# A prime-factor transform (3 by 256) in place of the half-length one, in an attention kernel that ends in a spectral convolution

## The chip, the cores and the metric

The kernel runs on one core of one Trainium2 chip. The metric is device microseconds for one execution; the time of a kernel is the median of its runs. The core has five engines that work side by side and wait for each other by semaphores: TensorE (PE; its weight loads are listed as PEld), VectorE (DVE), ScalarE (ACT), GpSimd (POOL) and SyncE (SP, which here only issues transfers). Matmul results land in an accumulator memory of eight banks of 512 fp32 columns (the tile `space` in the rows), from which VectorE and ScalarE copy them out.

## The reference

Attention with two kinds of heads, then a gated convolution over the sequence, done with Fourier transforms. Cut to what is computed:

```python
scores = q @ k.T / sqrt(64)                    # batch 4, 8 heads, 768 rows, 64 wide, fp32
mask = causal for some heads, else causal & (first 4 keys | last 64 keys)
x = softmax(where(mask, scores, -1e9)) @ v     # heads side by side: [4, 768, 512]
x1, x2, x3 = split(x @ w_proj, 3)              # each [4, 768, 512]
conv = irfft(rfft(x2, axis=1) * rfft(filter_fft, axis=0), n=768)
out = (x1 * conv * x3) @ w_out                 # [4, 768, 512]
```

## The kernel before

The function `patterned` names every small piece of work (an "op") and runs them in the order of a long text, `FAST`. A word of that text gives the op, the accumulator bank it starts in (`@0` to `@7`) and, where there is a choice, its engine (`/v` VectorE, `/s` ScalarE, `/p` GpSimd). Each engine executes its own ops strictly in that order; nothing is planned at run time. (`general`, a second program for other patterns of heads, is not taken.)

Heads are worked in sixteen pairs, n = 0 to 15, four to a batch b. For a pair: `lk`, `lq`, `lv` load (SP), `ck`, `cq`, `cv` cast to bf16, `T` and `E` transpose (for n below `TURNED` on TensorE and copied out by `E`, else by an SP transfer), `sc` makes scores in chunks, `ex` the exponential (ScalarE), `at` multiplies with the values, `rec` and `nm` normalise. The masks come in one of two ways: for n below `BIASED_FAST` an op `sb` adds a large negative number by a matmul of the identity with a table before `ex`; for the other pairs `mk` (and `mr`) multiply the exponentials by 0 or 1 on VectorE or GpSimd.

The forward transform is done before the projection, since both are linear. `fd` and `fe` fold the 768 rows to halves of 384 (difference and sum), `fA`, `fS`, `fb`, `fr` fold each half by three, and `W` multiplies with cosine and sine tables. `We` copies the result into `xh`, and `X` multiplies it with the middle third of `w_proj`: the spectrum of x2 in three tiles t of two times 512 columns. `Xe` copies it out, and `pa`, `pb`, `pc` multiply it by the filter's spectrum `HAB` into `P`; the third tile needs its halves of the partitions swapped, which `sw` does by two SP transfers. The filter's own spectrum comes from `fold`, `F` and the scaled copies `H`, with two SP transfers (`Hd`).

The inverse transform `c` has, for each of four blocks of 128 channels (cb), two sums of three products of 384 columns, one for even and one for odd frequencies. `ce` copies the first out, and two `cv` add and subtract to the two halves of the rows. `g` is x1 times x3, `y` the gate with conv, `o` the output product, `oe` its copy, `st` its store. `x1`, `x3` are the other two thirds of the projection, from the transposed attention output `xT` (`tn`, `te`: by TensorE for the pairs in `TURNED_BACK`, else by an SP transfer), and `xs` copies x1 out. `blank` ops are products of zeros that fill TensorE's time early on; there are thirteen of them (`BLANKS`), 29 products in the main text and the first five ahead of it.

Of the kernel before, what the change touches and what calls it, by code (L numbers as in the profile page):

```python
# [9 lines left out]
FP32 = mybir.dt.float32  # L10
# [103 lines left out]
SIXTHS = (0, 1, 2, 3, 4, 5, 6, 7, 8, 9, 10, 11, 12, 13, 14, 15)  # L114
# [7 lines left out]
lflag lk0 lq0 lk1 lq1 mblank want tcol fcol0 table sin0 fcol1 blank0@6 tfrac quarter mtab0 par turns other angle  # L122
ident mtab1 wrap size sin cos
# [3 lines left out]
ones1 ones2 mtab3 blank5@0 lq2 lk2 blank10@1 ck0/v skew0/s lv0 parb skew1/p G32/s T0.1@2 xp0 cq0/v lk3 blank6@3  # L127
mtab2 E0.1/v lv1 blank8@4 Gk1/s lv3 blank7@5 Gm00 btab G31/p blank1@6 ck1/v kz1 lq3 T0.0@7 lk4 alt blank3@0 Gm2
cq1/s G30/p Gh0 lq4 T1.1@1 Gm01 kz0 lv2 E0.0/s G00/v T1.0@3 G01/p Gm1 cq2/s lk6 E1.1/v sc0.1@4 sb0.1 lq6 ck2/p
sc0.3@6 ex0.1 Gh1 E1.0/v sc0.4@0 ones0 kx1/p sb0.4 lk5 sb0.3 T2.1@2 ex0.4 kz2 lk7 sc0.0@4 E2.1/v lq5 cv0/p sb0.0  # L130
Gt1@3 ex0.3 lq7 blank2@0 kx2/v Gt2@1 Gk0/p ex0.0 lv6 T2.0@2 ks1/p Ge2/v ck3/p sc0.2@6 Ge1/s E2.0/v sc1.2@4 sb1.2
lfilt sb0.2 T3.1@0 ex1.2 sc0.5@2 Gt0@1 ex0.2 cv1/v sc2.3@4 E3.1/v lv4 vx1/p sb0.5 ex0.5 sc1.0@6 lw2.1 Ge0/v
sb1.0 ks2/s vs1/v at0.0@2 lw2.0 ex1.0 at0.1 cq3/v lw0.1 T3.0@0 ex2.3 kx3/v sc1.1@6 rec0 lw1.1 sb1.1 nm0/v cv3/s
blank11@1 ex1.1 sc2.1@4 fe0/p sb2.1 tn0@1 cq4/v E3.0/s at1.0@2 lw0.0 blank9@6 ex2.1 ks3/v sc2.4@6 ck4/v at1.1
# [24 lines left out]
o0.1.1 o0.0.0 lk15 mk9.0/v ex10.0 sc9.2@2 o0.0.1 mk9.1/v T12 x11.2.0@4 ex9.2 mk10.0/v x11.2.1 fb7/v oe0.1/s
# [1682 lines left out]
```

## Time and profile before

| | |
|---|---|
| Runs | 195.18, 189.86, 193.86 us; median 193.86 |
| Profiled execution | 190.27 us, its span 188.4 us |
| Mean granted TensorE clock | 0.985 |
| Busy: TensorE, VectorE, ScalarE, GpSimd | 176.5, 161.2, 145.6, 69.0 us |
| Transfers | 34.01 MB, mean 180 GB/s |

Times in the rows are microseconds from the start of the span; a row of groups gives line, engine, operation, output<-inputs, shapes, count, then busy time, mean ns of one instruction, and the idle time of the engine just before them with what ended it. A matmul's mean duration is longer than its share of time, because the next one starts while it drains; the distance of starts tells the pace.

### The profile page before, as it was taken

The page shows a single profiled execution, that of the slowest core. Times are in us where ns is not written, and L with a number is a line of the kernel's source. Part 1 is how long each engine was busy: PE and PEld are TensorE (multiplying, and loading weights), DVE is VectorE, ACT ScalarE, POOL GpSimd, SP SyncE. Part 2 cuts the span into 40 slices and gives each one's busy share as a digit, 9 for nine tenths or more (in the row PEclk, how much of TensorE's full clock was granted, in tenths as well). Part 3 has the DMA queues.
Part 4 walks back from the last instruction along what each step waited for, and adds up shares of the span by engine and source line. Part 5 has one row for each costly group of instructions (what it writes and reads, how often), then busy time and mean ns, then how long its engine had stood idle before and what let it go on. Part 6 is the DMA issues. An engine that isn't in the chain of part 4 may idle for free.

```text
span 188.4 us, 4493 instructions
## 1 busy us (share of the span) xinstructions
PE 176.5 (94%) x1694; PEld 103.4 (55%) x1694; DVE 161.2 (86%) x329; ACT 145.6 (77%) x210; POOL 69.0 (37%) x103
## 2 busy tenths in 40 slices
PE   7879999989998999999999999999999999999970
PEld 2437664647745563575555656655657765555530
DVE  6887799789889999999989999999899996499810
ACT  5787899999999999988989999696977332426360
POOL 5874785554322224670250460700650630000000
PEclk9978999999999999999999999999999999999997
DMA  4999999999999999999999989982162002312074
GB/s 152 330 274 279 208 197 236 270 286 251 213 202 225 215 185 166 233 219 213 202 233 228 228 221 238 250 87 56 60 98 111 3 2 111 135 36 111 11 286 157
DMA packets 78955, 34.01 MB, mean 180 GB/s; under 512 B 68306, under 2 KB 75218, under 8 KB 78930
## 3 DMA queue, kind: packets, MB, share of 16 engines
q1 hardware_dynamic: 75986, 30.81, 73.9%
q0 software_dynamic: 2944, 2.88, 9.1%
q8 instruction: 14, 0.23, 0.5%
q14 instruction: 11, 0.09, 0.2%
HBM read 24.64 MB, written 6.29 MB: 164 GB/s over the span
## 4 chain that ended last, share of the span: by engine, by line
PE 66%; ACT 14%; DVE 6%; DMA 5%; issue 3%; POOL 2%; SPq 2%; DVEq 0%; ACTq 0%; POOLq 0%
PE space L1655 18%; PE space L1712 11%; PE space L1620 8%; PE space L1452 7%; PE space L1685 7%; PE space L1516 6%; ACT f_pT L1471 4%; DMA f_qkT<-f_qk_bf 3%; ACT f_HAB L1274 3%; DMA f_v_f<-in_v_dram 2%; PE space L1465 2%; ACT f_qk_bf L975 2%; SPq L1383 2%; PE space L1569 1%; PE space L1571 1%
## 5 line engine op out<-in xcount | busy, mean ns | idle before, releaser
L1471 ACT ACTIVATE f_pT<-space 128x1024 bf16<-128x1024 f32 (+3 forms) x68 | 58.8, 917 | 6.1 <-PE space L1465 1.9
L1655 PE MATMUL space<-f_xT,f_wproj 128*128 128x384 bf16 x256 | 47.9, 326 | 0.1
L1655 PEld LDWEIGHTS <-f_wproj 128*128 128x128 bf16 x256 | 24.0, 98 | 17.1 <-issue 1.0
L1712 PE MATMUL space<-f_wout,r_gy 128*128 128x512 bf16 x96 | 24.7, 379 | 0.0
L1452 PE MATMUL space<-f_qkT 64*128 64x128 bf16 (+3 forms) x248 | 22.6, 253 | 1.1 <-DVE f_attn L1533 0.5
L1620 PE MATMUL space<-f_wproj,f_xh 128*128 128x512 bf16 x96 | 22.7, 379 | 0.1
L1685 PE MATMUL space<-f_Gi,r_P 128*128 128x384 bf16 x96 | 19.0, 326 | 0.7 <-ACT f_evs L975 0.3
L978 DVE TENSOR_TENSOR f_pT<-f_pT,r_mtab 128x1024 bf16<-128x1024 bf16 (+3 forms) x33 | 18.5, 583 | 0.8 <-ACT f_pT L1471 0.6
L975 ACT COPY f_o<-space 128x1024 f32<-128x1024 f32 (+1 forms) x12 | 9.9, 836 | 11.3 <-PE space L1712 11.2
L1516 PEld LDWEIGHTS <-f_pT 128*128 128x128 bf16 x472 | 16.7, 97 | 3.6 <-issue 0.9
L1516 PE MATMUL space<-f_v_aug,f_pT 128*128 128x65 bf16 x392 | 17.9, 193 | 0.6 <-ACT f_X L975 0.5
L1452 PEld LDWEIGHTS <-f_qkT 64*128 64x128 bf16 x248 | 10.3, 94 | 13.1 <-issue 10.4
L978 POOL TENSOR_TENSOR f_uv<-f_fo 128x256 bf16<-128x256 bf16 x12 | 9.1, 766 | 21.1 <-DVE f_fo L978 15.8
L1696 DVE TENSOR_TENSOR f_conv<-f_evs,space 128x384 bf16<-128x384 f32 x32 | 16.1, 545 | 0.6 <-PE space L1685 0.3
L975 ACT CAST f_xh<-space 128x768 bf16<-128x768 f32 x14 | 11.2, 808 | 4.9 <-PE space L1573 4.6
L1620 PEld LDWEIGHTS <-f_xh 128*128 128x128 bf16 x96 | 9.0, 98 | 10.0 <-issue 0.4
L1712 PEld LDWEIGHTS <-r_gy 128*128 128x128 bf16 x96 | 9.0, 98 | 8.9 <-issue 0.4
L1533 DVE TENSOR_TENSOR f_attn<-space,f_rec 128x768 bf16<-128x768 f32 x14 | 13.4, 955 | 0.4
L1685 PEld LDWEIGHTS <-r_P 128*128 128x128 bf16 x96 | 8.8, 97 | 7.4 <-issue 1.1
L978 POOL TENSOR_TENSOR f_fo<-f_attn 128x384 bf16<-128x384 bf16 x11 | 10.4, 960 | 2.4 <-DVE f_attn L1533 1.9
L975 ACT CAST f_X<-space 128x1024 bf16<-128x1024 f32 x8 | 8.2, 1020 | 2.8 <-PE space L1620 2.7
L978 POOL TENSOR_TENSOR f_pT<-f_pT,r_mtab 128x512 bf16<-128x512 bf16 (+1 forms) x6 | 6.8, 1146 | 9.1 <-ACT f_pT L1471 9.1
(136 smaller groups left out, 345.7 us busy)
## 6 DMA issues: line engine op xcount, KB each, us to landing
f_v_f<-in_v_dram SPq DMA_DIRECT2D x32, 192.0 KB, 4.7
out_dram<-f_o SPq DMA_DIRECT2D x9, 512.0 KB, 3.1
r_qk_f<-in_k_dram SPq DMA_DIRECT2D x10, 192.0 KB, 4.4
r_qk_f<-in_q_dram SPq DMA_DIRECT2D x10, 192.0 KB, 5.0
r_qk_f<-in_k_dram SPq DMA_DIRECT2D x4, 384.0 KB, 11.3
r_qk_f<-in_q_dram SPq DMA_DIRECT2D x4, 384.0 KB, 6.1
f_qk_f<-in_q_dram SPq DMA_DIRECT2D x4, 384.0 KB, 5.8
f_qk_f<-in_k_dram SPq DMA_DIRECT2D x4, 384.0 KB, 6.6
```

Of the source, the lines that this page charges most:

```text
L975: nc.scalar.copy(out=out, in_=in_)
L978: (nc.gpsimd if now["engine"] == "p" else nc.vector).tensor_tensor(out, a, b, op)
L1274: nc.scalar.activation(out=out_(), in_=in_(), func=AF.Copy, scale=w / S)
L1452: nc.tensor.matmul(sc[:, bank, col:col + 128 * cnt], lhsT=keys, rhs=qkT(n)[rows, 0, 128 * i:128 * (i + cnt)], start=(col == 0 or not biase ...
L1471: nc.scalar.activation(out=pT(n)[:, c, :, 0:w], in_=held[f"sc.{n}.{c}"][:, :, 0:w], func=AF.Exp, scale=SCALE)
L1516: nc.tensor.matmul(att[:, hh, 65 * i:65 * i + 65], lhsT=pT(n)[:, c, bank, col:col + 128], rhs=values, start=(z == 0), stop=(z == len(here) ...
L1533: nc.vector.tensor_mul(attn(n).rearrange("p i hh d -> p hh i d"), rows[:, :, :, 0:64], held[f"rec.{n}"][:, :, :, None].to_broadcast([128, ...
L1620: nc.tensor.matmul(ps[:, u, :], lhsT=xh(b)[:, cc, chain, 128 * part:128 * part + 128], rhs=wproj()[:, cc, DM:2 * DM], start=(cc == 0), sto ...
L1655: nc.tensor.matmul(ps[:, s, 0:HS], lhsT=wproj()[:, cc, part * DM + cb * 128:part * DM + (cb + 1) * 128], rhs=xT(b)[:, cc, s * HS:s * HS + HS],
L1685: nc.tensor.matmul(ps[:, 0, 0:HS], lhsT=P(b)[:, t, u, ch], rhs=Gi()[:, tile_no], start=(m == 0), stop=(m == 2))
L1696: fn(conv[:, half * HS:half * HS + HS], held[f"evs.{b}.{cb}"], held[f"c_ps.{b}.{cb}.1"][:, 0, 0:HS])
L1712: nc.tensor.matmul(ps, lhsT=gy(b)[:, cb, i * 128:(i + 1) * 128], rhs=wout()[:, cb, :], start=(cb == 0), stop=(cb == NC - 1))
```

## The change

The two-halves structure of the inverse goes. The 768 rows are now seen as 3 by 256: row 3t + s belongs to class s, and the transform over 3 and the one over 256 are done one after the other. The pieces:

- `c` has three sums (one for each class) of two products of 256 columns, from six rows that new ops `q` recombine out of `P`: `qa`, `qs`, `qz`, `qb`, `qp`, `qm` (two inputs, 1024 elements), `qr`, `qh`, `qd` (scalings). `ce` and the sums `cv` go. For batches 0 to 2 (`DIRECT`) `y` reads the accumulator; for batch 3 one `cv` copies it to bf16 first, on ScalarE.
- Even and odd frequencies lie in separate halves of the partitions, so `sw` goes, and `xh` holds six groups of 128. The tables are made for this order of rows: `Gi` directly from cosines and sines instead of by transposes (`Gt`, `Ge`).
- The filter goes the way of the data: `fAF`, `fSF`, `fbF`, `frF`, products `K`, copies `Ke`, and transposes `F`; `HAB` is scaled out of these. `Hd` goes.
- x1 and x3 are read from the accumulator by class (a step of three), and outputs are stored to every third row.
- `BIASED_FAST` rises from 4 to 8: pairs 4 to 7 are masked by `sb` matmuls instead of `mk`. `TURNED_BACK` loses pair 14.
- `BLANKS` has nine entries: eight products of zeros fewer. A one-element GpSimd copy, `gate`, stands ahead of the filter's and weights' loads. The whole text `FAST` is in another order (not shown).

```diff
-TURNED_BACK = (0, 1, 2, 3, 4, 5, 6, 7, 14, 15)
+TURNED_BACK = (0, 1, 2, 3, 4, 5, 6, 7, 15)
-BIASED_FAST = 4
+BIASED_FAST = 8
-BLANKS = (5, 2, 2, 2, 2, 2, 2, 2, 2, 2, 2, 2, 2)
+BLANKS = (5, 2, 2, 2, 2, 2, 2, 2, 2)
+DIRECT = ((0, 0), (0, 1), (0, 2), (0, 3), (1, 0), (1, 1), (1, 2), (1, 3), (2, 0), (2, 1), (2, 2), (2, 3))
...
+    @op("gate")
+    def _():
+        nc.gpsimd.tensor_copy(out=buf("gate", [1, 1], FP32), in_=held["qk_f32.3"][0:1, 0, 0, 0, 0:1])
...
+    def spectrum(ps, u, uv, br, ch):
+        nc.tensor.matmul(ps[:, u, 0:256], lhsT=br[:, 1, u, ch], rhs=G()[:, 3 * u:3 * u + 2], start=True, stop=False)
+        nc.tensor.matmul(ps[:, u, 0:256], lhsT=uv[:, 2 * u, ch], rhs=Gk()[:, u], start=False, stop=True)
+        nc.tensor.matmul(ps[:, u, 256:384], lhsT=br[:, 0, u, ch], rhs=G()[:, 3 * u + 2], start=True, stop=True)
+
+    def sorted_(x, ps):
+        ev(x.rearrange("p g (u j) -> p u g j", u=2), ps[:, :, 0:HS].rearrange("p u (g j) -> p u g j", g=6))
...
+    sixths("F", fold, uvF, brF)
+    for cc in range(NC):
+        for u in range(2):
+            @op(f"K{cc}.{u}")
+            def _(cc=cc, u=u):
+                spectrum(banks(f"K_ps{cc}"), u, uvF(), brF(), slice(128 * cc, 128 * cc + 128))
...
+    for t in range(3):
+        @op(f"F{t}")
+        def _(t=t):
+            ps = banks(f"F_ps{t}", BF16, 1)
+            for c, g in enumerate(SPECTRUM[t]):
+                for cc in range(NC):
+                    nc.tensor.transpose(ps[:, 0, DM * c + 128 * cc:][:, 0:128], Hx()[:, cc, g], identity())
...
-        for half in range(2):
-            @op(f"sw{b}.{half}")
...
-                nc.sync.dma_start(out=Xw[to], in_=held[f"X.{b}.2"][at])
+        # qa: SD[0:2] = P1 + P2     qs: SD[2:4] = P1 - P2     qr: row 0 of SD = 2 * row 0 of four P rows
+        # qh: Y0 = P0 / 2           qz: Y0 += SD[0, 3]        qd: SD[1:3] *= sqrt(3)
+        # qb: P0 -= SD[0, 3]        qp: P[2:4] = P0 + SD[1:3] qm: P[4:6] = P0 - SD[1:3]
...
-                ev(buf(f"x1s.{b}.{cb}", [128, 2, HS], BF16, tag), held[f"x1_ps.{b}.{cb}"][:, :, 0:HS])
+                ev(buf(f"x1s.{b}.{cb}", [128, 3, 2, 128], BF16, tag), classes(held[f"x1_ps.{b}.{cb}"]))
...
-                    for m, (t, u, tile_no) in enumerate(INVERSE[r]):
-                        nc.tensor.matmul(ps[:, 0, 0:HS], lhsT=P(b)[:, t, u, ch], rhs=Gi()[:, tile_no],
-                                         start=(m == 0), stop=(m == 2))
+                for s, (re, im) in enumerate(POINTS):
+                    for c, rows in enumerate((re, im)):
+                        rhs = Gi()[:, c].rearrange("p a f -> p (a f)")[:, START[s]:START[s] + 256] if s else Gj()[:, c]
+                        nc.tensor.matmul(ps[:, 256 * s:256 * s + 256], lhsT=rows(b)[:, ch], rhs=rhs,
+                                         start=(c == 0), stop=(c == 1))
...
+                if (b, cb) in DIRECT:
+                    to = y if cb < NC - 1 else buf(f"conv.{b}.{cb}", [128, S], BF16, f"conv{cb % 2}")
+                    nc.vector.tensor_mul(to, held[f"c_ps.{b}.{cb}"].rearrange("p a f -> p (a f)")[:, 0:S], x)
```

The lines with `#` stand for the nine ops of the recombination.

More of the change, by code (lines that the diff above doesn't have):

```diff
@@ L130 @@
[L130 to L134, printed above, removed]
@@ L193 @@
+x13.3.0@6 pc3.0/v x33.0.0 qd3/p qh3/s x33.2.1@2 g3.0 x13.2.1 qb3/v x13.3.1 xs3.2/s qz3/v x33.1.0@4 xs3.3/s qm3/v
+x33.1.1 qp3/v x33.2.0 g3.1 c3.0@0 g3.2 c3.1@6 cv3.0/s c3.2@4 cv3.1/s y3.0/v c3.3@2 cv3.2/s y3.1/v x33.3.0@0
+cv3.3/s y3.2/v x33.3.1 y3.3/v o3.1.0@6 g3.3 o3.3.0@7 o3.1.1 o3.3.1 oe3.1/s o3.0.0@4 oe3.3/s st3.1 o3.0.1
+o3.5.0@5 oe3.0/s st3.3 o3.5.1 st3.0 o3.4.0@2 oe3.5/s o3.4.1 st3.5 o3.2.0@3 oe3.4/s o3.2.1 st3.4 oe3.2/s st3.2
 """
```

472 lines of the change are left out of this document (233 added, 239 removed).

## The prediction

> **What bounds the kernel now.** I read the page first, then busy time by stage, then the chain of work that ended last.
>
> ```profile
> span 188.4 us, 4493 instructions
> PE 176.5 (94%) x1694; PEld 103.4 (55%) x1694; DVE 161.2 (86%) x329; ACT 145.6 (77%) x210; POOL 69.0 (37%) x103
> ...
> 0.00:20.00 20.00, 17.10 (x130) 8.79 (x131) 15.43 (x40) 14.76 (x22) 13.82 (x37) 0.91 0.95 260
> 20.00:80.00 60.00, 56.65 (x669) 34.87 (x668) 54.61 (x110) 58.72 (x81) 27.26 (x35) 1.00 1.13 221
> 80.00:180.00 100.00, 100.00 (x886) 58.64 (x885) 90.43 (x180) 70.24 (x107) 27.89 (x33) 1.00 0.67 138
> 60.00:150.00 90.00, 89.08 (x895) 53.22 (x894) 86.09 (x182) 78.47 (x121) 33.15 (x37) 1.00 0.90 173
> ```
>
> The columns after the stretch's length are busy PE, PEld, DVE, ACT and POOL, then granted clock, DMA share and GB/s. There are three stages. Up to 20 us everything starts up. From 20 to 80 us ScalarE is busy 58.72 of 60 us and sets the pace; TensorE idles 3.35 us there. From 80 to 180 us TensorE is busy all the time, and only matmul columns count. A busy TensorE can still be slow, so I check its pace in the chain.
>
> ```profile
> 38.28 2.43 ACT f_pT L1471 x3
> ...
> 166.29 0.65 PE space L1655 x4
> 171.11 2.44 PE space L1685 x15
> 177.55 5.19 PE space L1712 x24
> ```
>
> In the chain the pieces from 30 to 49 us are nearly all ScalarE (the first row is the longest). Late, fifteen 384-column matmuls take 2.44 us (0.163 us each, 424 ps a column) and twenty-four of 512 columns take 5.19 us (0.216 us, 422 ps a column). Time is proportional to columns: this stage has nothing to give but columns. The last row ends it at 182.74 us, and 5.7 us follow for the last copy and store. The profiled execution took 190.27 us, 1.87 us outside its span.
>
> **The change part by part.**
>
> *Inverse transform (c).* Before: 96 products of 384 columns. After, by the order of the built program: 96 of 256 columns.
>
> ```profile
> 104.62 0.27 PE L1571 MATMUL space<-f_Gk,f_uv 128*128 128x256 bf16 x1
> 104.73 0.22 PE L1573 MATMUL space<-r_G,f_br 128*128 128x128 bf16 x1
> ...
> 10.00:80.00 70.00, 4.33 (x21) 1.80 (x21) 0.98 1.13 229
> 80.00:183.00 103.00, 14.72 (x75) 7.00 (x75) 1.00 0.67 142
> ```
>
> A 256-column product starts 0.11 us before its successor, so each saves 0.163 - 0.11 = 0.053 us, 5.1 us over 96. The last two rows are the inverse's own matmuls: 75 stand behind 80 us, where columns are time: -4.0 us. The other 21 (1.1 us) stand where ScalarE paces; I credit half, -0.5 (bounds 0 and -1.1).
>
> *Mask by matmul for heads 4 to 7.* The bias products double, and 13 mask multiplications go.
>
> ```profile
> L1465 PE MATMUL space<-f_btab,r_identity 128*128 128x128 bf16 (+2 forms) x33 | 6.5, 303 | 0.0
> L978 DVE TENSOR_TENSOR f_pT<-f_pT,r_mtab 128x1024 bf16<-128x1024 bf16 (+3 forms) x33 | 18.5, 583 | 0.8 <-ACT f_pT L1471 0.6
> 20.00:80.00 60.00, 2.39 (x8) 0.59 (x8) 1.00 1.13 221
> ```
>
> Cost on TensorE: 9,344 columns, 3.9 us at 422 ps, at most the 6.5 us busy of the first row. It falls between 20 and 80 us. What hides it: the 3.35 us idle there, 1.1 us of shorter inverse, and the eight removed blank products, which are just the eight blank products that the last row counts in this stretch (8 x 0.216 = 1.7 us). That is 6.2 us against 3.9 to 6.5, so I take 0. With the cover gone an exponential waits behind its bias product and ScalarE, the pacer, is late by up to 3.9 us. VectorE loses eleven masks, 11 x 0.56 = -6.2 us; GpSimd two.
>
> *Tables and filter.* Three groups of table transposes (18 products) go, and 18 filter products of 512 columns become 24 small spectrum products and 24 transposes.
>
> ```profile
> L1274 ACT ACTIVATE f_HAB<-space 128x1024 bf16<-128x1024 f32 (+2 forms) x6 | 5.1, 888 | 0.1
> L975 ACT CAST f_X<-space 128x1024 bf16<-128x1024 f32 x8 | 8.2, 1020 | 2.8 <-PE space L1620 2.7
> L975 ACT COPY f_evs<-space 128x384 f32<-128x384 f32 x14 | 6.8, 493 | 3.1 <-DVE f_conv L1696 2.2 <-PE space L1685 0.8
> L975 ACT CAST f_xh<-space 128x768 bf16<-128x768 f32 x14 | 11.2, 808 | 4.9 <-PE space L1573 4.6
> ```
>
> By columns 9,216 become 8,192: nothing. On ScalarE 5.1 us of scaled copies become four casts of 0.81 and three half-width scalings, half of the first row's largest (about 0.5 each): 4.7 us. Other small copies move both ways, so I take 0 (bounds -1.5 and +1).
>
> *Recombination (q).* Nine operations a batch are new; six are two-input operations of 1024 elements.
>
> ```profile
> L978 DVE TENSOR_TENSOR r_P<-r_P,f_m 128x1024 bf16<-128x1024 bf16 x12 | 8.2, 687 | 0.1
> L1696 DVE TENSOR_TENSOR f_conv<-f_evs,space 128x384 bf16<-128x384 f32 x32 | 16.1, 545 | 0.6 <-PE space L1685 0.3
> L978 DVE TENSOR_TENSOR r_gy<-f_conv,r_gy 128x768 bf16<-128x768 bf16 x10 | 5.7, 569 | 0.1
> L1674 DVE TENSOR_TENSOR r_gy<-r_x1s,space 128x768 bf16<-128x768 bf16 x8 | 7.5, 942 | 0.3 <-PE space L1655 0.3
> ...
> L978 DVE TENSOR_TENSOR f_uv<-f_fo x20: 277/287/871, 29.4 to 151.0; 128x256 bf16<-128x256 bf16 x20
> L1561 DVE SCALAR_TENSOR_TENSOR f_br<-f_uv,f_fo x16: 408/419/841, 32.1 to 156.2; 128x256 bf16<-128x256 bf16 x16
> ```
>
> Per batch VectorE loses eight sums of 0.545 and four gates of 0.569 (6.6 us) and takes 6 x 0.687 and four gates read straight from the accumulator at 0.95 (7.9 us): +1.3, or +5 over four batches. The filter's sixths add four operations on 1024 elements, 3 x 0.69 and one of the f_br kind four times as wide (4 x 0.42): +3.7. Against the masks (-6.2) and some copies moved off, VectorE's total stays about 161 us. ScalarE loses fourteen evs copies (6.8 us) and takes four conv copies and two or three 1024-wide scalings, some 6 us: even too.
>
> *Tail.* For the last batch the q chain stands between the last spectrum product and c3. In the new order TensorE has o2.5.1 and thirteen blocks of x1/x3 there, 0.22 + 13 x 0.65 = 8.7 us. After the last spectrum copy (f_X, 1.02 us) VectorE has three P and five q operations of 0.69, one small scaling and one gate of 0.95, with the copy about 8 us. Nearly level, so a slip shows. qd3 runs on GpSimd, and qm3 and qp3 wait for it.
>
> ```profile
> L1161 POOL TENSOR_SCALAR f_skew<-r_P 128x256 f32<-128x256 f32 x1 | 1.1, 1057 | 0.4 <-ACT r_P L1155 0.4
> L978 POOL TENSOR_TENSOR f_m<-f_X,f_HAB 128x1024 bf16<-128x1024 bf16 x1 | 2.1, 2123 | 3.5 <-DVE r_P L978 3.5
> ```
>
> Its 1024 elements are not in the trace: 1.06 us for 256 is the lower bound, four times that, 4.2 us, the upper. I take 2.1 us, the second row, one input more but the same width. The cover is pc, g, qb and qz, 3.0 us; so the tail costs 0 to 1.2 us from this and I put +0.5.
>
> *The rest.* g and xs now read the accumulator with a step of three.
>
> ```profile
> L971 DVE COPY f_qkT<-space 128x768 bf16<-128x768 bf16 x8 | 7.6, 950 | 0.9 <-PE space L1407 0.9
> L975 ACT COPY f_qkT<-space 128x768 bf16<-128x768 bf16 x8 | 6.2, 802 | 0.1
> ```
>
> The qkT copies read it with steps too and take 950 and 802 ns, what contiguous reads take (L1674's 942; f_xh's 808). So 0; at most 0.4 us each on 16 gates. Ten SP transfers (spectrum swap, filter halves) go; one transpose (tn14) leaves TensorE, six products, -0.3 us behind 80 us, for an SP transfer; only x1 and x3 of that batch read it. The gate copy on GpSimd stands ahead of the weight loads, but cq3, ahead of it, waits for the same load: 0. The whole order is dealt anew. As a check I add up both orders at these prices: behind the last exponential about 46 us of TensorE's columns stood before and 37 stand now, and ScalarE has some 3 us more to do up to it. By that path too the end comes 5 to 6 us earlier if ScalarE stays as full.
>
> **Sum:** 188.4 - 4.0 - 0.5 - 0.3 + 0.5 = 184.1 us of span, 186.0 us as its own time, 2.2% below 190.27. The three runs are 195.18, 189.86 and 193.86; the profiled one lies near their lower end. Scaled to their middle, 192.5: 192.5 x 186.0 / 190.27 = **188.2 us** (186 to 190 as the runs fall).
>
> **A rule weighed.** In the first of the 1 us stretches below TensorE is 54% busy; from 12 to 15 us, the other two and the one between them, its granted clock is 0.50.
>
> ```profile
> 9.00:10.00 1.00, 0.54 (x10) 0.37 (x8) 0.73 (x3) 1.00 (x2) 1.00 (x5) 1.00 1.13 348
> 12.00:13.00 1.00, 0.96 (x6) 0.46 (x6) 0.92 (x2) 0.18 (x2) 0.85 (x4) 0.50 1.18 299
> 14.00:15.00 1.00, 1.00 (x10) 0.73 (x9) 0.96 (x2) 1.00 (x3) 1.00 (x4) 0.50 1.28 211
> ```
>
> The Trainium skill (TensorE: Matmul & The Clock Gate, Part 1) has the clock halved only after an idle window of about 3.4 us; by that rule the removed blanks, in a stretch where TensorE never idles so long, cost nothing. The rows fit a milder cause, a half-busy stretch. The sum by either is the one above; what the rows add is rival 3.
>
> **The rivals.** (1) *Exponentials wait for the new bias products.* For: ScalarE 58.72 of 60. Against: the cover above. Price +3.9: 189.9 us own, 192.1 scaled. (2) *The first stage shortens too*, since heads 4 to 7 lose the mask between exponential and product, and VectorE the 6.2 us of them. Half of that and the other 0.5 of the inverse: 186.0 - 3.6 = 182.4, 184.5 scaled. (3) *The clock falls once more* without the blanks: 3 us at 0.50 as in those rows lose 1.5 us of work: 187.5, 189.7 scaled; against it, TensorE is busy 56.65 of 60 us there. (4) *VectorE becomes the bound, held by GpSimd*: the slower one. VectorE is busy 86.09 of 90 us from 60 to 150, 3.9 us free.
>
> In the f_uv and f_br rows above some two-input operations take 0.58 us more than their median (least/median/most in ns). Three batches' recombination lies in that stretch: 18 operations late by 0.58 are 10.4 us, and 3 x 1.3 = 3.9 more; perhaps seven of the eleven masks leave it (-3.9, an estimate) and 3.9 us are free. The other 6.5 show, and of the inverse's gain only the last batch's is left (24 x 0.053 = 1.3): 190.3 + 6.5 - 1.3 = 195.5 us own, 197.8 scaled. It decides once VectorE's net addition there passes 3.9 us. The Trainium skill (SBUF — State Buffer, Who interferes with whom) has a VectorE operation with two SBUF inputs contend with a GpSimd one that reads SBUF; the rows fit, and by that rule the new ones are exposed as the removed gates were.
>
> **How the numbers follow.** Forecast 0.47, rival 1 0.18, rival 2 0.13, rival 3 0.05, rival 4 0.17. About 2% is what a measurement of this kernel tells from no change; in its own time the lines are 186.5 and 194.1 us. The forecast (186.0) lies just under the first, so three quarters of it count as faster (0.36), with rival 2: 0.49, and 0.01 of rival 3. Rival 4, but for its mild end, is slower: 0.14. The rest, 0.36, is no change. The range 184.0 to 195.0 takes in the forecast with its costs' bounds, rivals 1 to 3 and the mild end of rival 4.
>
> **What would show it.** c matmuls with 75% or less of the old busy time; TensorE still busy 100% from 80 us on, and its last matmul near 178.5; ScalarE above 9.7 of 10 from 30 to 70 us; VectorE's sum near 161; q operations at 0.69; g and xs unchanged. Wrong if TensorE shows gaps over 2 us after 80 us, VectorE's two-input means rise above 0.8, or the first X0 product comes later than before.

## The result, and the profile after

The changed kernel takes 199.0 us, median of four runs, against 191.9 for four runs of the kernel before on the same chip: a ratio of 1.048 (95% interval 1.043 to 1.054). The forecast was 188.2. The profiled execution took 198.05 us, its span is 196.2, 7.8 more than before. Some executions in this study lose a few microseconds to a stall on a transfer and a lower clock at 30 to 45 us; the ratios leave the worst of them out (193.86 and 195.18 us of the kernel before, so that 1.048 is not 199.0 over 191.9), and the rows below are from executions without it.

First the page of the changed kernel, and its busy time by the same stretches as in the prediction (columns: length, PE, PEld, DVE, ACT, POOL, granted clock, DMA share, GB/s).

```profile
span 196.2 us, 4504 instructions
PE 175.9 (90%) x1725; PEld 106.7 (54%) x1725; DVE 165.6 (84%) x311; ACT 147.6 (75%) x201; POOL 82.6 (42%) x112
...
0.00:20.00 20.00, 15.91 (x115) 7.82 (x116) 15.69 (x40) 14.40 (x22) 16.14 (x41) 0.91 0.97 274
20.00:80.00 60.00, 54.51 (x686) 35.27 (x686) 53.87 (x96) 52.44 (x70) 26.72 (x32) 1.00 1.14 218
80.00:180.00 100.00, 94.57 (x864) 57.51 (x863) 89.83 (x166) 73.83 (x101) 39.72 (x41) 0.98 0.56 127
```

TensorE is busy for about as long as before (175.9, was 176.5), in spite of the narrower inverse; it idles 20.3 us in place of 11.9. ScalarE, which was to stay full from 20 to 80 us, is busy 52.44 of 60. From 80 to 180 us, where TensorE never paused before, 5.4 us are missing, and GpSimd works 13.6 us more over the whole.

A better cut than these stretches is at two marks: the first product of batch 0's spectrum (X0), and the last x1 or x3 product. These rows are the matmul rows of the two lines, with the start of the first and of the last product behind the three durations; the kernel before comes first (L1620 and L1655), then the changed one (L1628 and L1693).

```profile
L1620 PE MATMUL space<-f_wproj,f_xh x96: 376/379/390, 54.7 to 165.9; 128*128 128x512 bf16 x96
L1655 PE MATMUL space<-f_xT,f_wproj x256: 322/326/337, 42.0 to 177.2; 128*128 128x384 bf16 x128
```

```profile
L1628 PE MATMUL space<-f_wproj,f_xh x96: 376/379/390, 61.9 to 172.5; 128*128 128x512 bf16 x96
L1693 PE MATMUL space<-f_xT,f_wproj x256: 323/326/350, 49.7 to 185.2; 128*128 128x384 bf16 x128
```

Busy time in the three parts that these marks cut, before and then after:

```profile
0.00:54.70 54.70, 49.97 (x563) 30.13 (x563) 45.59 (x96) 48.66 (x66) 32.90 (x63) 0.97 1.09 243
54.70:177.20 122.50, 120.97 (x1108) 70.91 (x1107) 113.61 (x232) 93.40 (x140) 36.07 (x40) 1.00 0.76 152
177.20:188.40 11.20, 5.53 (x27) 2.31 (x24) 1.96 (x3) 3.58 (x6) 0.00 (x0) 0.89 0.52 191
```

```profile
0.00:61.90 61.90, 53.34 (x631) 33.46 (x632) 52.32 (x108) 51.26 (x72) 37.52 (x70) 0.97 1.10 239
61.90:185.20 123.30, 116.86 (x1072) 71.00 (x1071) 111.77 (x202) 92.86 (x124) 45.06 (x42) 0.99 0.61 134
185.20:196.20 11.00, 5.67 (x26) 2.26 (x24) 1.51 (x2) 3.48 (x7) 0.00 (x0) 1.00 0.39 147
```

The front, up to the first X0 product, is 7.2 us longer: TensorE is busy 3.4 us more there and idles 3.8 us more. The rows of L1655 and L1693 also place the delay: the first x1 or x3 product starts at 42.0 us before and at 49.7 us after, and from there to X0 it is 12.7 and 12.2 us, so all of it arises ahead of that product. The middle is 0.8 us longer although TensorE is busy 4.1 us less: it idles 6.4 us in place of 1.5. The end is the same. So two losses are to be explained, one in the front and one in the middle, and the second eats a gain that did come.

The middle points at a cause at once. GpSimd's part of the recombination, its rows of the changed kernel's line for scalings (least, median, most in ns), and the same kinds of scaling on VectorE and on ScalarE:

```profile
L1185 POOL TENSOR_SCALAR f_SD<-f_SD x2: 2772/2960/3147, 115.9 to 176.8; 128x1024 bf16<-128x1024 bf16 x2
L1185 POOL TENSOR_SCALAR f_SD<-r_P x1: 5362/5362/5362, 75.8 to 75.8; 1x2048 bf16<-1x2048 bf16 x1
L1185 POOL TENSOR_SCALAR f_Y<-r_P x1: 2769/2769/2769, 145.3 to 145.3; 128x1024 bf16<-128x1024 bf16 x1
```

```profile
L1183 DVE TENSOR_SCALAR f_Y<-r_P x2: 424/426/428, 72.0 to 124.5; 128x1024 bf16<-128x1024 bf16 x2
L1183 DVE TENSOR_SCALAR f_SD<-r_P x2: 681/681/681, 115.0 to 176.1; 1x2048 bf16<-1x2048 bf16 x2
...
L1187 ACT ACTIVATE f_SD<-f_SD x2: 1039/1048/1057, 81.1 to 147.1; 128x1024 bf16<-128x1024 bf16 x2
L1187 ACT ACTIVATE f_SD<-r_P x1: 1904/1904/1904, 144.4 to 144.4; 1x2048 bf16<-1x2048 bf16 x1
```

The one in 5.36 us is qr0, which doubles a single row of batch 0. What waits for it is in the timeline (start, duration, in brackets the idle time before and who ended it):

```profile
75.75 5.36 POOL L1185 TENSOR_SCALAR f_SD<-r_P 1x2048 bf16<-1x2048 bf16 x1 [11.65 <-DVE f_SD L975]
...
81.15 0.69 DVE L975 TENSOR_TENSOR f_Y<-f_Y,f_SD 128x1024 bf16<-128x1024 bf16 x1 [1.55 <-POOL f_SD L1185]
...
81.14 1.06 ACT L1187 ACTIVATE f_SD<-f_SD 128x1024 bf16<-128x1024 bf16 x1 [0.24 <-POOL f_SD L1185]
...
84.88 0.28 PE L1720 MATMUL space<-f_Gi,r_P 128*128 128x256 bf16 x1 [1.34 <-DVE r_P L975]
85.48 0.50 PE L1720 MATMUL space<-f_Gi,r_P 128*128 128x256 bf16 x3 [0.31 <-DVE r_P L975]
```

qz0 on VectorE and qd0 on ScalarE start in the 0.04 us behind it, the sums qm0 and qp0 follow, and the first inverse products, which read them, start late. From 82 to 87 us TensorE is idle for 3 of the 5 us.

### The profile page after: what moved, and what is told of

The parts are those of the page before. It is cut to its first block, busy times and chain, and to the rows that moved or that the text cites. A ratio compares the mean times of both kernels' runs of the same rounds, so it can differ in the third digit from the quotient of the medians.

```text
span 196.2 us, 4504 instructions
## 1 busy us (share of the span) xinstructions
PE 175.9 (90%) x1725; PEld 106.7 (54%) x1725; DVE 165.6 (84%) x311; ACT 147.6 (75%) x201; POOL 82.6 (42%) x112
## 5 line engine op out<-in xcount | busy, mean ns | idle before, releaser
L1693 PE MATMUL space<-f_xT,f_wproj 128*128 128x384 bf16 x256 | 45.9, 326 | 0.0
L1693 PEld LDWEIGHTS <-f_wproj 128*128 128x128 bf16 x256 | 24.2, 98 | 15.8 <-issue 0.2
L1628 PE MATMUL space<-f_wproj,f_xh 128*128 128x512 bf16 x96 | 23.5, 379 | 0.0
L972 ACT COPY f_o<-space 128x1024 f32<-128x1024 f32 (+1 forms) x15 | 12.6, 846 | 7.1 <-PE space L1746 7.0
L970 POOL COPY f_v_x<-f_v_aug 64x520 bf16<-64x520 bf16 (+1 forms) x15 | 9.6, 643 | 14.8 <-DVE f_v_aug L968 10.7
L975 POOL TENSOR_TENSOR f_fo<-f_attn 128x384 bf16<-128x384 bf16 x12 | 11.7, 981 | 6.0 <-DVE f_attn L1555 5.5
L1185 POOL TENSOR_SCALAR f_SD<-f_SD 128x1024 bf16<-128x1024 bf16 x2 | 5.9, 2960 | 19.3 <-DVE f_SD L1183 19.3
L1628 PEld LDWEIGHTS <-f_xh 128*128 128x128 bf16 x96 | 9.0, 97 | 9.3 <-issue 0.2
L972 ACT CAST f_xh<-space 128x768 bf16<-128x768 f32 x12 | 9.5, 802 | 5.0 <-PE space L1281 3.2
L1487 PE MATMUL space<-f_btab,r_identity 128*128 128x128 bf16 (+2 forms) x66 | 12.7, 290 | 0.0
L975 DVE TENSOR_TENSOR f_pT<-f_pT,r_mtab 128x512 bf16<-128x512 bf16 (+3 forms) x22 | 11.9, 560 | 0.2 <-ACT f_pT L1493 0.2
L1720 PE MATMUL space<-f_Gi,r_P 128*128 128x256 bf16 x64 | 10.3, 281 | 1.6 <-DVE r_P L975 1.6
L968 DVE COPY f_qkT<-space 128x768 bf16<-128x768 bf16 x9 | 8.4, 947 | 3.2 <-ACT f_pT L1493 2.5
```

Of the source, the lines that this page charges most:

```text
L970: nc.gpsimd.tensor_copy(out=out, in_=in_)
L972: nc.scalar.copy(out=out, in_=in_)
L975: (nc.gpsimd if now["engine"] == "p" else nc.vector).tensor_tensor(out, a, b, op)
L1487: nc.tensor.matmul(held[f"sc.{n}.{c}"][:, bank, 128 * at:128 * (at + width)], lhsT=identity(), rhs=btab()[:, what:what + width], start=Fal ...
L1628: nc.tensor.matmul(ps[:, u, :], lhsT=xh(b)[:, cc, SPECTRUM[t][u]], rhs=wproj()[:, cc, DM:2 * DM], start=(cc == 0), stop=(cc == NC - 1))
L1693: nc.tensor.matmul(ps[:, s, 0:HS], lhsT=wproj()[:, cc, part * DM + cb * 128:part * DM + (cb + 1) * 128], rhs=xT(b)[:, cc, s * HS:s * HS + HS],
```

## The experiments

All ratios are to the kernel before, run on the same chip in the same set; in brackets stands the 95% interval, and a point is one per cent of the time before, 1.9 us. "Head 4" stands for the pair n = 4, as in the prediction. Two theories stood at the start: A, GpSimd's scalings hold the chain; B, the loss is the fuller stage from 20 to 80 us, where the bias products now stand (rival 1).

**1. The four scalings off GpSimd** (`q_off_gpsimd`).

```
-qr0/p ... qd1/p ... qh2/p ... qd3/p
+qr0/v ... qd1/v ... qh2/v ... qd3/v
```

> The changed kernel with its four GpSimd scalings of the recombination (qr0 5.36 us, qd1 2.77, qh2 2.77, qd3 the fourth) on VectorE, where such ones take 0.68 and 0.43 us. Theory A, the GpSimd scalings hold the chain: behind qr0 TensorE idles 0.75 + 1.34 + 0.31 + 0.57 = 3.0 us between 83 and 87 us and then runs 5 us at a granted clock of 0.70 (1.5 us of work); behind qd1 and qh2 it idles 0.46 + 0.53 + 1.02 = 2.0. VectorE pays 0.68 + 3 x 0.43 = 2.0 us. So 4.5 to 6.5 us come back: ratio to the kernel before 1.014 to 1.025, and 80 to 90 us at clock 1.00 with TensorE above 9.5 of 10. Theory B, the loss is the fuller stage from 20 to 80 us (bias products, ScalarE short of scores from 50 to 60): under 2 us come back, ratio 1.037 or more.

Measured: 1.0138 (1.0061 to 1.0216). Theory A, with the most it had promised: 3.5 points of the 4.8 are these four instructions, 6.6 us of 191, by intervals that leave a point either way; by the marks the middle gets 5.3 us shorter (the table below). One sign was missed: from 80 to 90 us the clock is 1.00 as expected, but TensorE is busy 8.44 of 10 us (in the trace of run 6, which stands on this kernel) and not 9.5, so it still waits. VectorE's sums that read the scaled rows also get faster; the row of the changed kernel and that of run 6 (count, busy, mean ns, idle before):

```profile
L975 DVE TENSOR_TENSOR r_P<-r_P,f_SD 128x1024 bf16<-128x1024 bf16 x12 | 9.0, 772 | 0.8 <-POOL f_Y L1185 0.8
```

```profile
L975 DVE TENSOR_TENSOR r_P<-r_P,f_SD 128x1024 bf16<-128x1024 bf16 x12 | 8.0, 684 | 0.0
```

**2. Only the longest of them** (`qr0_only`: `qr0/p` becomes `qr0/v`).

> The changed kernel with qr0 alone, the one of 5.36 us, on VectorE. Theory A: its stall and the clock behind it, 3.0 + 1.5 us, less 0.7 on VectorE: 3 to 4.5 us back, ratio 1.024 to 1.033. Theory B: under 1 us, ratio 1.042 or more. If it gives as much as all four together, the other three cost nothing.

Measured: 1.0294 (1.0234 to 1.0353), theory A again: 1.9 points for qr0, so some 1.6 for the three others together, again within a point or so. By the marks qr0 is 2.6 us of the middle and the others 2.7.

**3. The bias alone, in the kernel before** (`bias_alone`).

```
-BIASED_FAST = 4
+BIASED_FAST = 8
-btab = C("btab", [128, 7, 128], BF16, "X1")
+btab = C("btab", [128, 7, 128], BF16)
-... sc4.0@2 ... ex4.0 ... mk4.0/v ...        (so for all of n = 4 to 7)
+... sc4.0@2 sb4.0 ... ex4.0 ...
```

> The kernel before with the mask of heads 4 to 7 put in by bias products (BIASED_FAST 8, the thirteen mask multiplications dropped, each bias product right behind its scores, the bias table in memory of its own), all else as before. Theory A: the bias is hidden as forecast, ratio 0.995 to 1.005. Theory B (rival 1 of the prediction): the exponentials wait for it, +2 to +3.9 us, ratio 1.010 to 1.020.

Measured: 1.0125 (1.0062 to 1.0188): theory B's number, 2.4 us (1.2 to 3.6), in an order that was not made for it and with the bias table moved, so what costs it isn't told apart.

**4. The eight blanks taken out of the kernel before** (`blanks_off`: the words `blank4`, `blank9`, `blank11` and `blank12` go).

> The kernel before without the eight blank products between 20 and 80 us, all else as before. Theory A and B: TensorE has idle time there, so 0 to -1 us, ratio 0.995 to 1.000. Rival, the clock needs them: a drop to 0.70 for some 5 us as in the changed kernel, +1.5 us, ratio 1.008, with the clock row of that stretch under 1.00.

Measured: 0.9998 (0.9945 to 1.0050). The blanks cost nothing and hold nothing, to half a point.

What stays behind experiment 1 is 1.4% above, where 2.2% below was forecast. The other runs go for these 3.6 points, first by parts of the order (theory C: work that is late in the first 50 us starves TensorE). All stand on the kernel of experiment 1.

**5. Masks again for heads 4 to 7** (`masks_back`: `BIASED_FAST = 4`, each `sb` of n = 4 to 7 dropped, `mk` and `mr` some six words behind their exponentials on VectorE).

> The changed kernel with the four scalings off GpSimd (ratio 1.0138 to the kernel before) and with heads 4 to 7 masked by thirteen multiplications on VectorE again instead of the bias products. Theory B, the bias products delay the exponentials here too (1.25% in the kernel before): 2 to 2.4 us back, ratio 1.001 to 1.004. Rival, hidden here, while VectorE pays its 6.2 us of masks (87.11 of 90 us busy from 60 to 150): ratio 1.014 or more.

Measured: 1.0479 (1.0422 to 1.0535), the rival and more: 3.4 points worse. That VectorE has no room for these masks where I put them is my reading; no run tells it from the order.

**6. Weights early** (`weights_early`).

```
-gate kx3/s lfilt ... lwo ... lw0.1 ... ck7/p ... lw2.0 ... lw1.1 ... lw2.1 ... lw0.0 ... lw1.0
+gate kx3/s lfilt ... lwo lw0.1 lw2.0 lw1.1 lw2.1 lw0.0 lw1.0 ... ck7/p
```

> The same kernel without GpSimd scalings, with its six projection-weight transfers issued on GpSimd's queue right behind the filter's and the output weights', where now five of them stand behind a copy that waits for k7 (issued at 31 to 39 us; the kernel before issued them at 19 to 25). Theory C, work that is late in the first 50 us starves TensorE (26.1 busy of 30 us from 20 to 50, 28.6 before): 1 to 2 us back, ratio 1.003 to 1.009. Rival, the weights aren't what TensorE waits for there, and take the q, k and v transfers' bandwidth: 1.014 or more.

Measured: 1.0112 (1.0050 to 1.0174), between the two.

**7. v2 early** (`v2_early`: the word `lv2` goes ahead of `lk4`).

> The same kernel without GpSimd scalings, with the v2 transfer issued ahead of k4, q4, q3 and q6. In its trace ScalarE waited 2.92 us for that transfer, TensorE idled 3.91 us behind it and the clock was 0.78, 0.50 and 0.70 in the 15 us that follow (5.1 us of work lost). Theory C: where this stall occurs 3 to 5 us go with it; it doesn't occur in every execution (the changed kernel's own trace has no such wait), so 1 to 2.5 us on the whole, ratio 1.001 to 1.009. Rival, the wait passes to q3, k4 or q6, which now come later: 1.012 to 1.018.

Measured: 1.0131 (1.0041 to 1.0221): no gain. In its trace VectorE waits 3.7 us for the filter's transfer instead.

**8. One filter scaling ahead** (`h_order`: `H0.1/v` goes ahead of `H2.1/v`).

> The same kernel without GpSimd scalings, with one filter scaling (H0.1) put ahead of three others on VectorE: it frees the bank that head 4's attention products wait for (0.95 us of weight load and 0.56 us of matmul waiting at 52.4 us, and an exponential 1.22 us behind). Theory, these waits count: 0.6 to 1.2 us back, ratio 1.008 to 1.011. Rival, another wait takes their place: 1.012 to 1.016.

Measured: 1.0091 (1.0053 to 1.0128), as expected, but within the error of no change from 1.0138.

**9. Is the inverse's gain there?** (`c_padded`)

```
 rhs = Gi()... if s else Gj()...
+if c == 0:
+    nc.tensor.matmul(ps[:, 256 * s:256 * s + 256], lhsT=rows(b)[:, ch], rhs=rhs, start=True, stop=True)
```

> The changed kernel without GpSimd scalings (ratio 1.0138), with one more product of 256 columns in each third of the inverse transform, overwritten by the next: 48 x 0.109 us = 5.2 us, what the inverse lost by its narrower products. It tells whether step 2 of the prediction holds (columns behind 80 us are time). Theory: 4 to 5.2 us more, ratio 1.034 to 1.042. Rival, these products stand where TensorE waits for something else: under 2 us, ratio 1.024 or less.

Measured: 1.0416 (1.0358 to 1.0473), 2.8 points or 5.3 us more for 5.2 us of products. The prediction's step on the inverse holds: columns in the middle are time.

**10. The mends together, and two more** (`mended`: 6, 7 and 8, and `qd0/s nm7/s` become `qd0/v nm7/v`), **11. x1 earlier** (`mended_x1`: `x10.3.0` right behind `x10.3.1@0`, `xs0.3/s` behind `cv6/s`, `sc5.0@0 sb5.0 ex5.0` behind `x10.1.1`, `sc7.0` in bank 2), **12. blanks** (`mended_blanks`: sixteen blank products ahead of `T4.0`, `tn0`, `tn1`, `T3.0`, `at2.1`, `T7.1` and `T5.1`).

> The changed kernel without GpSimd scalings, with the weights early, v2 early and H0.1 ahead (the three edits before, together), and with qd0 (1.09 us) and the twelve small normalisations nm7 (2.6 us) moved from ScalarE to VectorE, where they take 0.43 and 0.96: from 76 to 88 us ScalarE is full and TensorE waits for its exponentials, 2.9 us idle. Theory C, late exponentials starve TensorE: the parts add up, 2 to 3 us back, ratio 0.998 to 1.004. Rival, one wait takes the place of the other: 1.007 to 1.012.

> The kernel mended, and between 50 and 60 us, where ScalarE is busy only 6.16 of 10 us, the x1 block x10.3.0 done right behind its other half and copied at once, so that bank 0 comes free and head 5's scores and exponential go before the other x1 and x3 products. Theory C: 1 to 2 us of ScalarE's idle time are used, and the exponentials from 76 us on come sooner: 1 to 2 us less than mended. Rival: ScalarE's idle time there costs nothing, same as mended within 0.4%.

> The kernel mended, with sixteen blank products (3.5 us) in TensorE's gaps between 26 and 40 us, ahead of transposes and of attention products that wait for other engines. In three traces TensorE is about half busy from 26 to 36 us, and its clock then falls to 0.50 to 0.85, which loses 1.7 to 5 us of work. Theory, a half-busy stretch lowers the clock: it stays at 1.00 from 30 to 45 us, 1.5 to 3 us less than mended. Rival, the clock falls all the same or the blanks stand in the way: 0 to 2 us more than mended.

Measured: 1.0224 (1.0164 to 1.0283), 1.0346 (1.0254 to 1.0437) and 1.0266 (1.0175 to 1.0358). The first two miss theory and rival: the parts don't add up, and the x1 block ahead makes it worse. In the trace of 10 VectorE is busy 10.00 of 10 us from 80 to 90, where ScalarE was relieved, but by the marks the middle is only 0.5 us longer than in run 6 and the front 1.1 us, so why the parts don't add up isn't shown. The third gives its rival's time, 0.8 us more than mended: the clock does stay higher with the blanks (0.83 in place of 0.66 from 30 to 40 us), and the time doesn't follow.

Then by leaving parts out (theory D: the recombination on VectorE is the bound; B again; F: the filter).

**13. Without the recombination** (`no_q`: the words `qa`, `qs`, `qr`, `qz`, `qd`, `qb`, `qp`, `qm` go).

> The changed kernel without GpSimd scalings (1.0138), with the recombination left out but for the halving qh (qa, qs, qr, qz, qd, qb, qp and qm of all four batches; the inverse reads the plain products instead). VectorE loses 6 x 0.68 + 0.68 + some 0.4 = 5.2 us a batch, ScalarE 1.0. Theory D, the recombination on VectorE is what takes the inverse's gain back: 5 to 8 us less, ratio 0.972 to 0.988. Rival, VectorE's q operations are hidden and the order starves TensorE: 1 to 2 us less, 1.003 to 1.009.

Measured: 1.0089 (1.0049 to 1.0130): 0.5 points. VectorE falls to 147.3 us busy, and the kernel hardly notices: the rival, at the least gain that it allowed.

**14. Heads 4 to 7 without bias or mask** (`no_bias47`: `biased = n < 4 and ...`, the fifteen words `sb4.0` to `sb7.2` go).

> The changed kernel without GpSimd scalings, with heads 4 to 7 neither masked nor biased (their 33 bias products, 9,344 columns, 3.9 us, left out). Theory B, they delay the exponentials: 2 to 3.9 us less, ratio 0.993 to 1.003. Rival, hidden in TensorE's gaps: under 1 us, 1.009 to 1.014.

Measured: 1.0174 (1.0075 to 1.0273). No gain; the interval leaves room for a point. So the cost that the bias has in the order of the kernel before does not show in this one, and is ruled out only in part.

**15. Less on VectorE** (`light_vector`: 6 and 8, and `ck9`, `ck11`, `fe6`, `vx7`, `vs7`, `vs9` from `/v` to `/p`).

> The changed kernel without GpSimd scalings, with the weights early (1.0112 alone) and H0.1 ahead (1.0091 alone), and six small operations between 63 and 90 us moved from VectorE to GpSimd, which is nearly idle there: ck9, ck11, fe6, vx7, vs7 and vs9, together some 2.1 us of VectorE. Theory D, VectorE is the bound from 75 to 90 us: 1 to 2 us less than the two edits before would give, ratio 0.996 to 1.003. Rival, GpSimd's slower copies (0.4 to 0.9 us each) or its hold on VectorE cost what is saved: 1.006 to 1.012.

Measured: 1.0121 (1.0035 to 1.0207). The rival: VectorE full is not VectorE the bound. Theory D falls with 13 and 15.

**16 and 17. Head 3 ahead of head 4** (`head3_first`, `head3_rows`).

```
-sc4.0@6 ... sc4.2@2 ... sc4.3@6 ... sc4.5@2 ... sc4.1@0 ... sc4.4@2 ... sc3.1@0 ... sc3.2@2 ... sc3.0@6 ... at3.0@2
+sc3.1@6 ... sc3.2@2 ... sc3.0@6 ... sc4.0@2 ... at3.0@6 at3.1 sc4.2@0 ... sc4.3@2 ... sc4.5@0 ... sc4.1@2 ... sc4.4@6 ... at4.0@2
```

> The changed kernel without GpSimd scalings, weights early and H0.1 ahead (1.009 to 1.011 each alone), with head 3's scores, exponentials and attention products put ahead of head 4's, its copies and row transform brought forward with them, and head 4's attention products then ahead of head 5's scores; everything else in the order of the changed kernel. Theory E, the order feeds batch 0 too late: ScalarE's idle time from 50 to 60 us (3.8 us) shrinks and the stage behind it has its products, 2 to 4 us back, ratio 0.988 to 1.000. Rival, this order is no limit either: 1.006 to 1.012.

> The kernel head3_first, with the row transforms of heads 2 and 3 (their sixths and W2, W3) brought forward too, so that batch 0's first X product can come sooner than 61 us. Theory E: another 0.5 to 1.5 us, ratio 0.982 to 0.996. Rival: the same as head3_first within 0.4%, since X0 also waits for head 5's attention products, which stand ahead of it on TensorE.

Measured: 1.0417 (1.0367 to 1.0468) and 1.0536 (1.0490 to 1.0581), 3 and 4 points worse. The edits did not do what they were to do: X0 starts at 64.9 and 68.5 us, not sooner. So they don't refute that a sooner X0 would help; they show what a later one costs. Of the second:

```profile
L1628 PE MATMUL space<-f_wproj,f_xh x96: 377/379/390, 68.5 to 174.1; 128*128 128x512 bf16 x96
L1693 PE MATMUL space<-f_xT,f_wproj x256: 322/326/337, 55.4 to 186.8; 128*128 128x384 bf16 x128
```

**18. Without the filter's transform** (`no_filter`: the words `fold0`, `fold1`, `fSF`, `fAF`, `fbF`, `frF`, all `K`, `Ke`, `F` and `H` go; three memsets of the table stand at `fold0`).

> The changed kernel without GpSimd scalings (1.0138), with the filter's transform left out: its folds, sixths, spectrum products, copies, transposes and scalings; the filter's table is set to a constant by three VectorE memsets instead, so all later work stays as it is. TensorE loses 8,192 columns (3.5 us), ScalarE four casts of 0.80 and four scalings of 0.59 (5.6 us), VectorE some 10 us, all between 37 and 53 us. Theory F, the filter holds that stage, where it delays head 4's attention products and batch 0's first x1 and X products: these come 4 us sooner or more, and the end with them, 4 to 6 us, ratio 0.982 to 0.993. Rival, the filter is hidden as forecast and only the dealing of the rest counts: under 2 us, 1.003 or more.

Measured: 1.0155 (1.0120 to 1.0190), the rival. The memsets took 1.76 us each on VectorE, 5.3 of the 10 us that it was to save, so the run is weaker than planned; but ScalarE's 5.6 us and TensorE's 3.5 were really gone, and neither the first x1 product (49.9 us) nor X0 (61.3) moved. One thing weakens it more: the granted clock was 0.84 from 40 to 50 us, where run 6 had 1.00, which may hide up to 1.6 us.

Laid side by side by the two marks, the runs say more than one by one. Rows of four of them, in this order: weights early (6), padded inverse (9), no recombination (13), no filter (18).

```profile
L1628 PE MATMUL space<-f_wproj,f_xh x96: 377/379/390, 61.4 to 166.7; 128*128 128x512 bf16 x96
L1693 PE MATMUL space<-f_xT,f_wproj x256: 322/326/337, 49.3 to 179.4; 128*128 128x384 bf16 x128
```

```profile
L1628 PE MATMUL space<-f_wproj,f_xh x96: 377/379/390, 61.5 to 170.1; 128*128 128x512 bf16 x96
L1693 PE MATMUL space<-f_xT,f_wproj x256: 322/326/337, 49.4 to 184.1; 128*128 128x384 bf16 x128
```

```profile
L1627 PE MATMUL space<-f_wproj,f_xh x96: 376/379/390, 61.2 to 165.7; 128*128 128x512 bf16 x96
L1692 PE MATMUL space<-f_xT,f_wproj x256: 322/326/337, 48.9 to 178.3; 128*128 128x384 bf16 x128
```

```profile
L1626 PE MATMUL space<-f_wproj,f_xh x96: 377/379/390, 61.3 to 166.6; 128*128 128x512 bf16 x96
L1691 PE MATMUL space<-f_xT,f_wproj x256: 323/326/337, 49.9 to 179.3; 128*128 128x384 bf16 x128
```

| kernel | front: first X0, us | middle: to the last x1 or x3, us | ratio |
|---|---|---|---|
| before | 54.7 | 122.5 | 1 |
| changed | 61.9 | 123.3 | 1.048 |
| qr0 off GpSimd | 62.0 | 120.7 | 1.029 |
| all four off, weights early | 61.4 | 118.0 | 1.011 |
| the four off, no recombination | 61.2 | 117.1 | 1.009 |
| the four off, no filter | 61.3 | 118.0 | 1.016 |
| the four off, inverse padded | 61.5 | 122.6 | 1.042 |
| head 3 first | 64.9 | 118.0 | 1.042 |
| head 3 first, rows | 68.5 | 118.3 | 1.054 |

In every run without the GpSimd scalings the middle is 117.9 to 118.8 us whatever was done to the front, but for three: 117.1 without the recombination, 121.6 with the masks back (5) and 122.6 padded. 118.0 is 4.5 less than before, which is the size of the gain forecast for the inverse, and the padding gives 4.6 of it away. The 4.5 is not the inverse alone, though. By columns at 422 ps the inverse's 5.2 us leave the middle and so do some 1.6 us of scores and attention products (29 exponentials stand ahead of the mark now, for 27), some 0.9 us of bias products come in, and TensorE idles 2.9 us in place of 1.5. So it is the padded run, not the 4.5, that shows the gain. The front is 61.2 to 61.5 us in the four rows that have all four off and keep its order, and longer where I dealt it otherwise. (The ratios come from several executions and the marks from one, so they agree to about a point only.)

## Why the prediction was wrong, step by step

The budget by the marks is 7.2 (front) - 4.5 (inverse) + 5.3 (GpSimd scalings, 123.3 - 118.0) - 0.2 (end) = +7.8 us, the difference of the spans. Two terms of the sum failed, and each alone would have turned the sign.

- **Inverse, -4.5: right**, with the padded run's 4.6. Six products of 256 columns start 0.65 us apart, 0.109 each, as these rows of the changed kernel's timeline show:

```profile
181.43 0.38 PE L1720 MATMUL space<-f_Gj,f_Y 128*128 128x256 bf16 x2
181.64 0.60 PE L1720 MATMUL space<-f_Gi,r_P 128*128 128x256 bf16 x4
182.09 0.38 PE L1720 MATMUL space<-f_Gj,f_Y 128*128 128x256 bf16 x2
```

  The padded run shows that they are time. The sign to look for held as well: the busy time of the c products fell to 71%, as their line over the whole span shows, before (L1685) and then after (L1720):

```profile
0.00:189.00 189.00, 19.05 (x96) 8.80 (x96) 0.98 0.83 180
```

```profile
0.00:197.00 197.00, 13.46 (x96) 9.26 (x96) 0.98 0.75 167
```

- **Recombination on GpSimd: the first step that failed.** The step "Tail" priced qd3 alone, at 2.1 us from a two-input row, within bounds of 1.06 and 4.2; it took 3.15. The other three, qr0, qd1 and qh2, stood in the order with `/p` and have no term in the sum at all. I had asked of each what VectorE pays, and not what the chain waits for. The four together cost 3.5 points. In the tail, where the term stood, qd3 was hidden: TensorE ran x1 and x3 products without a pause from 172.98 us until the first c product of batch 3 at 181.43, and qd3 was done at 179.97.
- **Recombination on VectorE, +1.3 a batch and covered: right.** All of it costs 0.5 points, which is within the error.
- **"The rest ... the whole order is dealt anew": the second step that failed.** It was put at nothing, and its check by sums came out at 5 to 6 us sooner "if ScalarE stays as full". ScalarE didn't, and the first X0 product came 7.2 us later, which the prediction had named as a sign of being wrong. Adding up two orders at the price of each row tells what must be done, not what has to wait in a fixed order. Ahead of the first x1 or x3 product, where the delay arises, all 96 transposes of q and k stand now, for 66 before, and TensorE has some 4,350 columns more in all (1.8 us at 422 ps). ScalarE has 7.0 us more there, which is the size of the delay, but that sum doesn't explain it either: without the filter (18) it has 4.0 us less, and the product starts at 49.9 us all the same. Busy time up to that product, of the kernel before, the changed one and run 18:

```profile
0.00:42.00 42.00, 37.95 (x410) 21.49 (x410) 34.60 (x76) 36.17 (x48) 27.67 (x55) 0.96 1.07 247
```

```profile
0.00:49.70 49.70, 41.70 (x489) 26.04 (x490) 41.23 (x87) 43.21 (x62) 30.60 (x61) 0.97 1.08 244
```

```profile
0.00:49.90 49.90, 40.11 (x441) 23.20 (x442) 39.44 (x81) 39.22 (x55) 29.53 (x61) 0.93 1.08 250
```

- **Bias, 0: undecided.** Busy time of the bias products alone up to X0, before and after:

```profile
0.00:54.70 54.70, 6.54 (x33) 2.30 (x33) 0.97 1.09 243
```

```profile
0.00:61.90 61.90, 11.23 (x58) 3.70 (x58) 0.97 1.10 239
```

  Twenty-five more of them stand in the front, 7,168 columns or 3.0 us. All of the front's columns grew by 1.6 us only, since blanks and filter gave some back; the rest of TensorE's 3.4 us is a slower pace. Its idle time there did not shrink to take the bias in: cover that was counted as free was not free. One part of it was not there at all: the 1.1 us of shorter inverse was counted between 20 and 80 us, and in the new order the first c product starts at 83.17. Alone in the kernel before the bias costs 2.4 us. Yet leaving it out of the changed order gave nothing back, to a point. The masks that it replaces would cost more there (5).
- **Filter 0, blanks 0, reads with a step of three 0: borne out**, the first two by runs 18 and 4 to the error, the third by these rows (942 and 811 ns before, for the same operations):

```profile
L1712 DVE TENSOR_TENSOR r_gy<-r_x1s,space 128x768 bf16<-128x768 bf16 x8 | 7.6, 946 | 0.5 <-PE space L1693 0.5
L972 ACT CAST r_x1s<-space 128x768 bf16<-128x768 f32 x7 | 5.7, 808 | 1.1 <-PE space L1693 1.1
```

- **`gate`, 0:** the weights behind it came 10 us later than before (the last issued at 35 us, not 25; run 6 puts them back), for 0.3 points, which is no more than the error.
- **Rival 4** gave nearly the right time (195.5 us own, 198.05 measured) and the right culprit, GpSimd, by the wrong mechanism, so that its nearness is luck. VectorE was held a little: the sum qb0, which started at 81.75 us beside a copy on GpSimd, took 1.11 us in place of 0.68, and all twelve sums of the row under run 1 lost 1.0 us, not 0.58 each. What cost the time was that VectorE, ScalarE and TensorE waited for GpSimd's result. Rival 2's shorter first stage is refuted, it is 7.2 us longer. Rival 3's clock did fall once more, but behind qr0's stall and not for want of blanks (4).

What stays open is why the front takes 61.3 us. It is not the recombination or the weights' transfers, since neither moved it, and probably not the filter, with the reserve made under 18. For the bias it is undecided. The two orders of heads that I tried made the front longer, so the link that sets it wasn't found, and no kernel run here beats the one before.

## What to carry to other kernels

When a new chain of small operations is dealt over several engines, price every one on the engine that its word names, and ask what waits for it, not only what its engine has free: here one row of 2048 elements on the slowest engine cost 2.6 us by the marks and 3.6 by the ratios. In a program whose order is fixed, idle time is not a store that new work can be put into, and a sum of prices over a new order bounds it from below only; find the first instruction of the next stage (here X0) and forecast when it can start. Cutting a span at such marks separated a gain that came as forecast from two losses, where busy sums had mixed all three.

## What the runs showed of the hardware that was not expected

- **GpSimd's price went by the elements in a partition, not by the number of partitions.** A scaling of one partition by 2048 took 5.36 us, of 128 by 1024 2.77 to 3.15: 2.6 to 3.1 ns for each element of a partition. VectorE takes 0.68 and 0.43 for the same, ScalarE 1.90 and 1.05. The Trainium skill (GPSIMD Engine Reference, 3.1 Elementwise) has 769 ns for its best loop over 512 elements, from which 2048 would be an estimated 3.1 us; the 5.36 us measured are 1.7 times that best case.
- **The clock fell without a long idle window.** In the changed kernel's windows of 1 us, where the first column is busy PE:

```profile
82.00:83.00 1.00, 0.42 (x3) 0.13 (x2) 1.00 (x2) 1.00 (x2) 0.32 (x1) 1.00 1.20 231
83.00:84.00 1.00, 0.38 (x2) 0.10 (x1) 1.00 (x4) 0.11 (x1) 0.00 (x0) 1.00 1.26 198
84.00:85.00 1.00, 0.12 (x1) 0.10 (x1) 1.00 (x4) 0.69 (x4) 0.00 (x0) 1.00 1.54 229
...
86.00:87.00 1.00, 0.45 (x15) 0.45 (x16) 1.00 (x4) 1.00 (x6) 0.69 (x2) 1.00 1.08 241
87.00:88.00 1.00, 1.00 (x20) 1.00 (x16) 1.00 (x2) 1.00 (x2) 1.00 (x2) 0.52 1.05 223
88.00:89.00 1.00, 1.00 (x21) 1.00 (x20) 1.00 (x3) 1.00 (x2) 0.86 (x3) 0.50 0.18 37
```

  The longest idle time in it is the 1.34 us shown above. TensorE is busy 2.0 of the 5 us from 82 to 87, and 3 us at half clock follow. The rule weighed in the prediction, the Trainium skill's (TensorE: Matmul & The Clock Gate, Part 1), by which an idle window of about 3.4 us does it, would alone leave the clock at 1.00 here; the trace disagrees, as the first 15 us of the kernel before did. The same part of that page also tells of a kernel whose clock went back and forth because TensorE idled for short times often, and the rows fit that; it names no share, and no run here fixes one.
